# New instruction orders for a fused attention and channel-mixing kernel whose five engine queues are written out as lists

## Chip, cores and metric

The kernel runs on one core of one Trainium2 chip. The metric is the device time of one execution in microseconds (us). TensorE (PE in the profile) multiplies matrices, VectorE (DVE), ScalarE (ACT) and GpSimd (POOL) work elementwise, SyncE (SP) issues nearly all DMAs. Each engine executes its own instruction stream strictly in order; semaphores hold an instruction back until what it reads is there and what it overwrites is no longer needed.

## The reference, cut

```python
B, H, S, D = 8, 8, 576, 64          # batch, heads, positions, head width
scores = matmul(q, k.T) / sqrt(D)
cum = cumsum(log(clip(f, 1e-4, 1)), axis=-1)
scores = where(causal, -1e9, scores + cum[..., :, None] - cum[..., None, :])
attn = softmax(scores)
x = matmul(attn, v)                 # heads side by side: (8, 576, 512)
h = relu(x.T @ w_tok1) @ w_tok2     # mixing over positions, 576 -> 256 -> 576
u = x + h.T
out = u + relu(u @ w_ch1) @ w_ch2   # mixing over channels, 512 -> 1536 -> 512
```

The weights come as 64-bit floats and are turned into pairs of 32-bit parts on the chip ("decoded"). Where the kernel multiplies in the fast 32-bit format it splits a number into a high part and a low rest and adds three products.

## The kernel before

**Attention.** The 64 heads are handled one after the other, two of them (a pair) sharing their loads. Of a pair, q and k come by one DMA (line 670, tile `raw`), and POOL splits them: high part (line 650) and low part (line 658), both into the tile `hl`, of which there is one. SP then gathers each head's operands out of `hl` by three DMAs (lines 713 to 715, recorded as L705, `k<-hl`, 288 KB each): one needs the high part alone, two need both. Two small DMAs a head (line 699, `k<-cc`) add the rows of the running sums. PE makes the score products of 576 positions in three steps (line 732, 754), each into PSUM; DVE adds the mask and takes the extreme (line 739), ACT makes the exponentials (line 746), DVE the reciprocals of the sums (lines 764, 767), POOL divides, five instructions a head (line 774), PE transposes the result (line 788), ACT and DVE copy it out of PSUM in high and low parts (lines 419, 428), one part by way of POOL (line 422), and PE multiplies by the values (lines 856 to 868). The values of a pair come by a DMA (line 678, tile `vr`, two of them), split by ACT (line 648) and POOL (line 658 again, tile `vv`). The first eight heads take shorter ways: their q and k are used unsplit.

**Mixing.** After four heads and after eight of a batch, PE transposes their outputs and mixes over positions (lines 1365 to 1433), and after eight it does the first 256 of the 1536 hidden channels (lines 1463 to 1498), storing `u` (line 1443) and partial sums (line 1498, `pd<-part`) to device memory. These steps are interleaved with the attention of the next heads. After the attention (from about 575 us on) the weights of the other 1280 hidden channels are decoded, mostly on DVE (lines 519 to 579), and multiplied: for 768 tokens directly (lines 1032 to 1068), for the others by a scheme that saves products (lines 1172 to 1292).

**The order.** `build` makes 6091 steps, numbered as they are made; a step is a few instructions of one engine. `ORDER` holds, for each of the five engines, the numbers of its steps in the order in which it executes them (`16:31` is the 31 steps from 16 on). `Plan.run` goes through the five lists with the planner's own costs (`LAT`, the durations given to `op`); a step is taken when it is next on its engine's list, what it reads is there, and a free buffer of each kind that it needs is found. The costs decide which buffer or PSUM bank of a kind a step gets; what each engine does after what is the list's alone. Kinds in `FIFO` are handed out in the order of the steps' numbers.

**Steps that the text names.** 2: the zero row on POOL (line 456). 0 and 1: constant rows on POOL (lines 475, 478). 4, 5, 7: clip, logarithm and running sum of `f` (DVE, ACT, DVE; lines 458, 459, 463). 8, 9: ACT issues the rows of sums of the first two heads (line 443). 10, 11: split of the sums on DVE (lines 468, 469). 16 to 51: filler products of PE (line 491). 53, 54, 55: load, first activation and first DVE step of the first decoded weight tile; 63, 68: steps of the second. 189: load of the first head. 190, 193, 198 and 225, 228, 233: score products of the first two heads; 194, 195, 229, 230: extremes for them; 203, 204: the first head's reciprocals. 612, 613: the first split of q and k on POOL (high, low); 2073, 2074 the one of a later pair, and 1913, 2077 low splits of values. For the pair of 2073: 2078, 2079 small DMAs, 2080, 2081, 2082 gathers (2080 of the high part alone) of its first head; 2124, 2125 and 2126, 2127, 2128 those of its second; 2091, 2086, 2083 the first head's score products.

Of the kernel before, what the change touches and what calls it, by code (L numbers as in the profile page):

```python
# [28 lines left out]
        16:31 198 193 190 47 233 228 48:4 225 266 271 217 212 215 210 219 308 263 303 220:2 252 222 300 247 250 245 254 377 290 255:2 372 285 288 257 283 369 416 421 292 413 293:2 322 327 400 397 389  # L29
        325 295 392 460 329 463 468 320 330 512 331 433 332 507 334 404 337 405 504 436 444 406 441 407 340 480 343:2 448:2 483 491 345 622 630 346 488 625 347 450 348 451 676 668 357 495 353 496 532  # L30
        497 527 498 351 535 671 524 359 539 645 723 642 540:2 728 720 542 653 650 774 688 545 657 548 658 769 696 766 699 691 659 551 660 740 554:5 847 703 559 743 855 850 704:2 751 706 748 562 755
        564 896 786 789 756 901 757 893 568 797 758 570 867 794 948 945 953 583 801 870 802:2 584 804 579 878 875 580 587 994 588 882 913 883 916 924 999 884 991 885 593 598 921 603 608 928 968 929
        976 973 575 965 930:2 807 576 1109 810 980:2 1117 1011 1112 596 1019 1014 982 1022 983 1163 1155 1158 813 816:2 591 1026 1129 1027 1137 1140 1207 1028 1132 818 1029 1215 1210 1175 819:3 601
        606 1144:2 1256 1261 1253 826 832 1032 1035 1038 830 1146 1178 1147 1186 824 1183 1041 1227 1042 1342 1043 1190 1337 1334 1044:2 1238 1191 1046 1235 1230 1192:2 1273 1388 1049 1055 1242 1380
        1276 1284 1243 1383 1281 1244 1051 1057 1245 1070 1066 1440 1354 1432 1288:3 1357 1291 1362 1067 1365 1071 1481 1486 1478 1435 1400 1074 1369 1075 1403 1411 1370 1062 1371 1408 1372 1294 1297
        1063 1452 1415:2 1463 1417 1455 1460 1604 1418 1599 1300 1596 1303:2 1650 1467 1645 1468 1501 1469 1305 1470 1306 1506 1509 1307 1498 1308 1642 1616 1078 1513:2 1627 1624 1619 1083 1515 1697
        1702 1516 1085 1313 1694 1662 1631:2 1665 1670 1748 1673 1633 1080 1743 1740 1319 1519 1088 1093 1634 1317 1714 1311 1090 1677 1522 1725 1717 1678 1095 1829 1722 1525 1679 1821 1680 1824 1528
        1875 1529 1760 1530 1867 1729 1531 1763 1771 1730 1532 1768 1731 1533 1732 1870 1841 1542 1536 1775 1538 1852 1844 1544 1922 1776 1927 1849 1777 1919 1778 1557 1553 1968 1554 1558 1973 1856
        1965 1890 1898 1887 1857:3 1895 1549 1939 1550 1561 1902 1781 1942 1950 1903 1562 1947 1904 1784 1905 2091 2086 1787 2083 1790:2 2137 2132 1954 1792 1996 1955 1793 1956 1794 1988 1993 1957
        1795 1985 2129 2103 1565 2000:2 2114 2111 2106 2002 1572 2184 2189 2003 1570 1800 2181 2149 2118:2 2152 2160 2157 2235 2120 1567 2230 2227 1806 2006 1575 1580 2121 1577 2201 1804 1798 2164  # L40
        2009 2204 2212 2165 1582 2316 2209 2012 2311 2166 2308 2167 2015 2247 2362 2016:3 2216 2019 2250 2258 2217 2354 2255 2218 2020 2219 2357 2328 2023 2029 2262 2025 2331 2339 2031 2414 2263 2409
        2336 2264 2044 2265 2406 2040 2455 2041 2045 2460 2343 2452 2377 2374 2344 2385 2345:2 2382 2036 2426 2037 2048 2389 2268 2437 2429 2390 2049 2434 2391 2271 2392 2573 2578 2274 2570 2277:2
        2624 2619 2441 2279 2475 2442 2280 2443 2281 2480 2483 2444 2282 2472 2616 2590 2052 2487:2 2601 2598 2593 2057 2489 2676 2490 2671 2059 2287 2054 2668 2636 2722 2717 2062 2605 2067 2639 2714
        2647 2291 2606 2064 2644 2607 2285 2608 2293 2688 2493 2496 2069 2651 2499 2652 2691 2803 2699 2696 2653 2795 2654 2798 2734 2502:2 2849 2504:2 2703 2506 2737 2745 2704 2841 2742 2705 2507
        2706 2844 2815 2510 2516 2749 2512 2818 2826 2518 2901 2750 2896 2823 2751 2531 2752 2893 2527 2942 2528 2532 2947 2830 2939 2864 2872 2831 2523 2832 2869 2833 2524 2535 2861 2755 2876 2536
        2924 2916 2877 2758 2921 2878 2913 2879 3065 3060 2761 3057 2764:2 3106 3111 2928 2766 2970 2929 2767 2930 2768 2962 2967 2931 2769 2959 3103 3077 2541 2974:2 3088 3085 3080 2546 2976 3158
        3163 2977 2544 2774 3155 3123 3092:2 3126 3131 3209 3134 3094 2539 3201 3204 2780 2980 2551 2554 3095 2549 3175 2778 2772 3138 2983 3186 3178 3139 2556 3290 3183 2986 3140 3282 3141 3285 2989
        3336 2990 3221 2991 3328 3190 2992 3224 3232 3191 2993 3229 3192 2994 3193 3331 3302 2997 3003 3236 2999 3313 3305 3005 3388 3237 3383 3310 3238 3018 3239 3380 3014 3429 3015 3019 3434 3317
        3426 3359 3348 3351 3318:3 3356 3022 3400 3023 3363 3010 3411 3403 3242 3364 3011 3408 3365 3245 3366 3552 3547 3544 3248 3251:2 3593 3598 3253:2 3415 3590 3449 3416 3457 3417 3255 3454 3418
        3256 3446 3026 3033 3461 3031 3567 3261 3575 3462 3650 3572 3463 3642 3464 3645 3028 3036 3265 3267 3038 3564 3610 3696 3579 3467 3580 3688 3613 3618 3581 3621 3691 3582 3041 3662 3259 3043  # L50
        3470 3473 3777 3625 3769 3673 3665 3626 3772 3627:2 3670 3476 3815 3477 3818 3478:2 3823 3480 3677 3481 3711 3678 3719 3679:2 3486 3484 3716 3492 3723 3490 3800 3792 3724 3708 3797 3725 3875
        3870 3867 3726 3505 3501 3506 3502 3509 3804 3510 3838 3846 3805 3789 3843 3921 3806 3835 3807 3916 3913 3887 3515 3520 3850 3497 3898 3890 3729 3851 3498 3732 3852:2 3895 3513 3518 3933 3902
        3735 3936 3903 3944 3904 3941 3905 3738 3523 3528 3530 3739 3948 3740 3949 3741 3950 3742 3951 3743 3525 3748 3754 3954 3957 3960 3752 3746 3963:6 3971 3977 3973 3979 3984 3988 3996 3992 3989
        3985 3997 3993 4000 4005 4010 4017 4015 4012 4007 4002 4468 4474 4471 4480:2 4477 4482:3 4486 4485 4487 4494 4491 4495:4 4488 4499:3 4505 4512:4 4502 4508:4 4519 4516 4522:9 4533 4536:9 4547
        4550:9 4561 4564:8 4578:8 4572 4575 4586 4589 4592:9 4603 4606 4609 4612 4615 4618 4621 4665 4668 4671 4677 4686 4680 4689 4674 4692 4698 4707 4701 4710 4713 4722 4683 4695 4719 4704 4728
        4716 4725 4731 4734 4737 4740 4743 4749 4746 4752 4755 4758 4761 4764 4804 4767 4808 4812 4816 4820 4831 4835 4839 4843 4847 4856 4860 4864 4868 4872 4880 4884 4888 4892 4911 4896 4915 4919
        4937 4923 4941 4927 4945 4949 4953 5029 5032 5035 4968 5038 4972 5041 4976 5050 4980 5044 4984 5047 5053 5056 5059 5062 5065 5071 5068 5074 5077 5080 5083 5086 5089 5092 5095 5098 5101 5104
        5107 5110 5113 5116 5119 5122 5125 5128 5168 5131 5172 5176 5180 5195 5184 5199 5203 5220 5207 5224 5211 5228 5244 5232 5248 5236 5252 5275 5256 5279 5260 5283 5301 5287 5305 5291 5309 5394
        5313 5332 5317 5336 5397 5340 5400 5344 5403 5348 5406 5409 5415 5412 5418 5421 5424 5427 5430 5433 5436 5439 5442 5445 5448 5451 5454 5457 5460 5463 5466 5469 5472 5475 5478 5481 5484 5487
        5490 5493 5541 5496 5545 5549 5568 5553 5572 5557 5576 5593 5580 5597 5584 5601 5617 5605 5621 5609 5625 5648 5629 5652 5633 5656 5674 5660 5678 5664 5682 5766 5686 5705 5690 5709 5769 5713  # L60
        5772 5717 5775 5721 5778 5781 5787 5784 5790 5793 5796 5799 5802 5808 5805 5811 5814 5817 5820 5823 5826 5829 5832 5835 5838 5841 5844 5850 5847 5853 5856 5859 5862 5865 5905 5868 5909 5932
        5913 5936 5917 5940 5921 5944 5957 5948 5961 5981 5965 5985 5969 5989 5973 5993 6012 5997 6016 6038 6020 6042 6024 6046 6028 6050 6054 6081:2
    """,
# [1683 lines left out]
```

## Time and profile before

| | |
|---|---|
| three runs | 1071.07, 1073.4, 1081.29 us; median 1073.4 |
| profiled execution | 1076.76 us, of it 1075.0 us from the first to the last instruction |
| PE busy | 1032.4 us (96%) |
| DVE, ACT, POOL busy | 869.5, 643.1, 501.3 us |
| mean granted TensorE clock | 0.998 of full speed |

The span is the part of the execution that the profile records; the rest lies around it. A busy PE includes small waits inside its pipeline. In a row such as `[1.90 <-DMA k<-hl]` the engine stood idle for 1.90 us before the instruction and what ended that was a DMA.

### The profile page before, as it was taken

To read this page: it belongs to the slowest core of one execution; us is meant where nothing else is said; L and a number is where in the kernel's file an instruction comes from. 1 tells how busy PE (TensorE), PEld (TensorE's weight loads), DVE (VectorE), ACT (ScalarE), POOL (GpSimd) and SP (SyncE) were. 2 spreads that over 40 slices of the span, in tenths; PEclk is the share of its full clock that TensorE was granted. 3 is DMA by queue.
4 is the path that set the end of the run, shared out by engine and by line. 5 is a ranking of instruction groups with operands and counts; after the bars stand their busy time and mean duration, and the time that the engine had idled before them with its cause. 6 is when DMAs were issued, how large, how long until landed. Compare 5 with 4: busy or idle time off the path is not lost.

```text
span 1075.0 us, 20358 instructions
## 1 busy us (share of the span) xinstructions
PE 1032.4 (96%) x6374; PEld 908.7 (85%) x6374; DVE 869.5 (81%) x2112; ACT 643.1 (60%) x1604; POOL 501.3 (47%) x581
## 2 busy tenths in 40 slices
PE   8997899999999999989899999999999999999998
PEld 5576789899999998989898888878888888888887
DVE  7689888888878877768779899966995995797586
ACT  5778678888788887868778544422631541362142
POOL 6778877867868687768671200002521101102000
PEclk9999999999999999999999999999999999999999
DMA  4548677877777778676864699899899889879874
GB/s 134 158 109 213 170 188 170 255 172 197 197 195 208 179 182 211 155 191 174 218 192 169 217 322 308 270 311 326 281 344 348 239 269 344 282 223 342 244 203 144
DMA packets 138020, 243.36 MB, mean 226 GB/s; under 512 B 20757, under 2 KB 70677, under 8 KB 136889
## 3 DMA queue, kind: packets, MB, share of 16 engines
q1 hardware_dynamic: 137904, 242.05, 77.0%
q8 instruction: 51, 0.84, 0.3%
q14 instruction: 57, 0.46, 0.1%
q10 hardware_dynamic: 8, 0.01, 0.0%
HBM read 145.24 MB, written 46.66 MB: 179 GB/s over the span
## 4 chain that ended last, share of the span: by engine, by line
PE 58%; DMA 14%; DVE 12%; POOL 5%; SPq 4%; ACT 4%; issue 3%; DVEq 0%; POOLq 0%; ACTq 0%
DMA k<-hl 10%; PE bank L1176 5%; PE bank L1178 5%; PE bank L1177 5%; PE bank L732 4%; PE bank L788 4%; PE bank L1242 3%; PE bank L1243 3%; PE bank L1241 3%; PE pair L1241 2%; PE pair L1242 2%; PE pair L1243 2%; PE pair L732 2%; SPq L705 2%; POOL hl L658 2%
## 5 line engine op out<-in xcount | busy, mean ns | idle before, releaser
L774 POOL TENSOR_SCALAR pr<-pr,rec 128x192 f32<-128x192 f32 (+4 forms) x320 | 170.9, 552 | 45.6 <-DVE rec L767 27.0
L419 ACT ACTIVATE p<-bank 128x384 fp32r<-128x384 f32 (+3 forms) x300 | 130.2, 475 | 54.7 <-PE bank L788 50.2
L788 PE MATMUL bank<-ident,pr 128*128 128x128 f32 (+1 forms) x960 | 138.8, 275 | 6.7 <-DVE p L428 1.4
L746 ACT ACTIVATE pr<-bank,nmin 64x64 f32<-64x64 f32 (+3 forms) x256 | 118.4, 469 | 19.2 <-DVE nmin L739 13.4
L428 DVE TENSOR_TENSOR p<-bank,p 128x384 fp32r<-128x384 f32 (+1 forms) x180 | 105.8, 595 | 27.4 <-ACT p L419 26.0
L788 PEld LDWEIGHTS bank<-ident,pr 128*128 128x128 f32 (+1 forms) x960 | 106.7, 131 | 19.8 <-POOL pr L774 4.4
L739 DVE CUSTOM_DVE_ANT_0 bank<-bank,mask 128x448 f32<-128x448 f32 (+3 forms) x256 | 106.3, 433 | 21.1 <-PE bank L732 18.9
L732 PE MATMUL bank<-k 128*128 128x320 f32 (+1 forms) x448 | 79.4, 299 | 13.2 <-DMA k<-hl 10.7
L732 PEld LDWEIGHTS bank<-k 128*128 128x128 f32 x448 | 66.1, 176 | 26.2 <-DMA k<-hl 8.4
L658 POOL TENSOR_TENSOR hl<-raw,hl 128x1152 fp32r<-128x1152 f32 x28 | 74.7, 2667 | 1.0
L868 PE MATMUL pair<-p,vv 128*128 128x512 f32 x240 | 75.0, 318 | 0.0
L419 ACT ACTIVATE hid<-h 128x480 fp32r<-128x480 f32 x76 | 45.7, 606 | 47.7 <-PE bank L1242 27.5
L866 PE MATMUL pair<-p,vv 128*64 128x512 f32 x240 | 71.2, 337 | 0.0
L422 POOL TENSOR_SCALAR p<-low 64x576 fp32r<-64x576 f32 x60 | 41.0, 683 | 58.5 <-DVE low L428 27.3
L1016 POOL TENSOR_TENSOR d_raw<-d_raw 128x256 f32<-128x256 f32 x4 | 2.9, 735 | 122.3 <-DMA d_raw<-ud 122.3
L428 DVE TENSOR_TENSOR low<-bank,p 64x64 fp32r<-64x64 f32 (+1 forms) x120 | 51.8, 441 | 9.7 <-ACT p L419 8.5
L419 ACT ACTIVATE ring<-bank 128x288 fp32r<-128x288 f32 (+2 forms) x96 | 46.7, 498 | 17.4 <-PE bank L1398 5.5
L1194 ACT ACTIVATE h<-bank 128x480 f32<-128x480 f32 x19 | 10.9, 573 | 75.6 <-PE bank L1178 75.6
L425 POOL TENSOR_TENSOR ring<-xt,ring 128x576 fp32r<-128x576 f32 x32 | 46.2, 1453 | 20.8 <-ACT ring L419 20.5
L739 DVE CUSTOM_DVE_ANT_0 pair<-pair,mask 128x576 f32<-128x576 f32 x64 | 48.9, 765 | 8.5 <-PE pair L732 7.4
L419 ACT ACTIVATE st<-h 128x480 fp32r<-128x480 f32 x64 | 38.1, 604 | 23.7 <-PE bank L1242 8.6
L658 POOL TENSOR_TENSOR vv<-vr,vv 128x640 fp32r<-128x640 f32 x30 | 46.9, 1564 | 10.4 <-ACT vv L648 4.9
(357 smaller groups left out, 3466.1 us busy)
## 6 DMA issues: line engine op xcount, KB each, us to landing
pw<-wd SPq DMA_DIRECT2D x280, 256.0 KB
k<-hl SPq DMA_DIRECT2D x168, 288.0 KB
raw<-in_qk SPq DMA_DIRECT2D x28, 576.0 KB
vr<-in_v SPq DMA_DIRECT2D x32, 320.0 KB
d_raw<-in_w_ch SPq DMA_DIRECT2D x80, 128.0 KB
ud<-xt SPq DMA_DIRECT2D x8, 1152.0 KB
pd<-part SPq DMA_DIRECT2D x32, 288.0 KB
wd<-pw SPq DMA_DIRECT2D x20, 384.0 KB
```

Of the source, the lines that this page charges most:

```text
L419: nc.scalar.activation(out, in_, func, scale=scale)
L428: nc.vector.tensor_tensor(out, in_, asf(hi), op=ALU.subtract)
L658: (nc.gpsimd if eng == "POOL" else nc.vector).tensor_tensor(out, in_, asf(hi), op=ALU.subtract)
L732: nc.tensor.matmul(ps[:m, of : of + w], k[:, 0 if fq else 1, i0 : i0 + m], k[:, 1 if fq else 0, j0 : j0 + w], start=(x == 0), stop=(fq or ...
L739: nc.vector.tensor_tensor_reduce(x, x, E["mask"][:m, a : a + w], -1.0 / D**0.5, 3e38, op0=ALU.add, op1=ALU.min, accum_out=E["nmin"][sm][:m ...
L746: nc.scalar.activation(at(pr)[:m, poff[t] : poff[t] + w], at(buf)[:m, of : of + w], AF.Exp, bias=E["nmin"][sm][:m, t : t + 1], scale=-1.0, ...
L774: nc.gpsimd.tensor_scalar(x, x, r, 0.0, op0=ALU.mult, op1=ALU.add)
L788: nc.tensor.transpose(out, at(pr)[:, poff[i] + start[j] : poff[i] + end[j]], E["ident"])
L866: nc.tensor.matmul(x[:D], at(vv)[:, v0 + j, :D], at(pb)[:, 1, c0 : c0 + w], start=False, stop=last)
L868: nc.tensor.matmul(x, at(vv)[:, v0 + j, :], at(pb)[:, 0, c0 : c0 + w], start=False, stop=last)
L1176: nc.tensor.matmul(o, wt[:, 0, :], h_, start=(first and k == 0), stop=False, skip_group_check=True)
L1177: nc.tensor.matmul(o, wt[:, 1, :], h_, start=False, stop=False, skip_group_check=True)
```

## The change

Only the five lists in `ORDER` are different; steps, tiles, buffers, costs and every other line are the same, and each list holds the same numbers as before. Of PE's 1453 steps 743 stand at another place (by at most 22 places), of DVE's 1782 steps 1048 (at most 39), of ACT's 1284 steps 792 (at most 26), of POOL's 576 steps 439 (at most 17), of SP's 996 steps 702 (at most 71). From PE's step 5110 on (about 830 us) nothing is moved. The beginnings of the lists, and on POOL and SP the lines with steps 2073 to 2128:

```diff
     PE="""
-        16:31 198 193 190 47 233 228 48:4 225 266 271 217 212 215 210 219 308 263 303 220:2 252 222 300 247 250 245 254 377 290 255:2 372 285 288 257 283 369 416 421 292 413 293:2 322 327 400 397 389
...
+        16:36 193 190 198 228 233 225 266 271 217 212 263 215 210 219 303 308 220:2 250 222 300 247 252 245 372 377 254 369 255:2 290 285 257 288 283 416 421 292 413 293 327 294 325 295 322 320 392
...
     DVE="""
-        4 7 55:3 64 10 65:2 59 68 73 199 74:2 194:2 191 200 234:2 11 203 77 204 229:2 226 218 82 267 272 91 268 238:2 83 273 216 84 92 264 304 309 86 93 276 310 277 305 253 251 301 95 100:2 313:2 291
...
+        4 7 55:3 10 64:2 59 66 194 191 199 73 200 74 229 195 75 234:2 68 230 203:2 77 226 11 267 272 218 273 82 238:2 83 216 264 268 84 304 309 91 305 92:2 86 251 95 276 310 277 301 253 373 378:2 109
...
     ACT="""
-        5 54 63 8:2 60 72 69 196 192 201 197 202 236 232 81 231 237 78 214 213 90 227 211 269 275 270 6 274 265 312 311 223 87 249 248 306 246 307 99 302 96 108 380:2 286 258 287 375:2 371 364 419
...
+        5 8:2 54 63 60 72 192 201 196:2 202 237 78 231:2 69 236 227 81 213 275 214 6 274 269 211 270 90 265 306:2 311:2 302 87 223 96 249 248 99 108 246 381 380 375:2 114 371 105 258 287 286 420 284
...
     POOL="""
-        0:3 12 58 67 61 13 76 14 70 205 207:2 206 209 15 79 240:2 85 242 244 243 94 282 280 278:2 281 88 97 316 319 103 612 317:2 315 112 386:2 384:2 388 365 115 106 430 429 403 431 428 432 456 121
...
-        2074 1934:5 1901 1980:5 1953 2077 2171:2 2098:5 1999 2117 2144:5 2298 2175 2299 2163 2196:5 2242 1809 2243 1803 2215 2244:2 2396 2246 2397 2323:5 2261 2302 2369:5 2342 2028 2034 2560 2400
...
+        2 0:2 12:3 58 61 67 76 207 206 208 205 209 70 79 244 242 15 241 243 240 85 94 279 612 280 88 282 97 278 281 112 103 115 318 316 319 106 388 317 315 387 385 384 386 365 613 121 432 429 403 428
...
+        1758 1909:2 1815 1840 1836:2 1774 1839 1316 1838 1322 1882 1885 1883 1855 1886 1541 1547 1884 2073:2 1934:2 1901 1938 1937 1936 1913 1980 1984 1981 1953 1982:2 2171:2 2101 2098 2102 2100 2099
...
     SP="""
-        3 53 52 62 71 189 224 80 262 260:2 89 188 298:2 297 611 368 367 98 107 366 410:2 259 412 363 619 116 457 617 459 125 665 663 458 134 454 618 503 501:2 666 621 620 709 143 664 667 614 715 152
...
-        1865:2 1864 1092 1097 1914:3 2075 2072 1917:2 1960:5 1548 2078:3 2173 2124:3 2170 2081:2 2127:2 2176:2 2300 2178 2297 2179:2 2222:2 2225:2 2224 1574 2303:3 2398 1569 2349:2 2395 2306:2 2351:3
...
+        3 53 189 52 224 62 71 611 262 260:2 80 297 299 298 188 259 89 368 98 366:2 107 412 618 411 410 457 116 458 363 459 503 125 502 134 454 619 501 666 621 663 620 667 617 143 709 664 614 665 712
...
+        1820 1864 1819 1862 1908 1865:2 1863 1813 1915 4064 1911 1914 1916:3 1962:2 1961 1964 1960 2072 1087 1097 1092 2075 2080 2126 2079 2128 2125 2081 2127 2124 2078 2082 2170 1548 1082 2178:2
```

On POOL's list of before, 2073 and 1913 stand just ahead of the line that begins with 2074. Loads of q and k are 1908, 2072 and 2170 there, loads of values 1911, 2075 and 2173, stores 1082 to 1097.

## Rows read from the trace of the kernel before

**Rows 1.** The page: busy time of each engine, and the granted TensorE clock in 40 slices.
```profile
PE 1032.4 (96%) x6374; PEld 908.7 (85%) x6374; DVE 869.5 (81%) x2112; ACT 643.1 (60%) x1604; POOL 501.3 (47%) x581
...
PEclk9999999999999999999999999999999999999999
```
**Rows 2.** Windows: stretch, its length, busy us (and instructions) by engine, clock, DMA share, GB/s.
```profile
0.00:25.00 25.00, 20.73 (x128) 13.01 (x129) 18.43 (x58) 12.55 (x34) 16.12 (x28) 1.00 0.51 144
25.00:150.00 125.00, 112.70 (x698) 85.87 (x697) 102.58 (x305) 92.19 (x267) 101.81 (x125) 1.00 0.63 160
150.00:200.00 50.00, 48.64 (x376) 45.87 (x374) 43.26 (x126) 40.61 (x113) 39.92 (x48) 1.00 0.80 200
200.00:560.00 360.00, 347.38 (x2633) 327.38 (x2633) 283.04 (x838) 284.34 (x796) 270.81 (x329) 1.00 0.75 191
...
615.00:700.00 85.00, 83.47 (x480) 73.42 (x479) 83.38 (x190) 39.01 (x74) 0.00 (x0) 1.00 0.91 298
```
**Rows 3.** PE's waits from 200 to 560: total us, times, longest.
```profile
PE bank L732 <- DMA k<-hl: 10.2, 13, 1.9
```
**Rows 4.** PE's waits from 25 to 200, the longest in total.
```profile
PE bank L1397 <- DVE ring L428: 1.7, 1, 1.7
```
**Rows 5.** Timeline of the first 27 us: start, duration, engine, line.
```profile
3.84 1.36 POOL L475 MEMSET xt<- 2x1152 f32 x1 [1.79 <-DVE xt L1650]
...
4.23 0.68 ACT L459 ACTIVATE xt<-xt 64x576 f32<-64x576 f32 x1 [2.20 <-DVE xt L458]
...
5.13 1.05 POOL L478 MEMSET xt<- 2x1152 f32 x1
...
6.24 0.58 POOL L456 MEMSET xt<- 64x576 f32 x1
...
6.47 3.70 PE L491 MATMUL pair<-ident 128*64 128x48 f32 x60
6.85 1.35 DVE L463 TENSOR_TENSOR_SCAN cc<-xt 64x576 f32<-64x576 f32 x1 [2.66 <-POOL xt L456]
...
8.23 1.84 ACTq L443 DMA_DIRECT2D xt<-cc  x2
...
11.39 2.11 PE L732 MATMUL bank<-xt 128*128 128x320 f32 x8 [1.22 <-DVE d_g L531]
```
**Rows 6.** Timeline of POOL around 450 us.
```profile
447.85 1.15 POOL L650 TENSOR_SCALAR hl<-raw 128x1152 fp32r<-128x1152 f32 x1
448.97 1.54 POOL L658 TENSOR_TENSOR vv<-vr,vv 128x640 fp32r<-128x640 f32 x1
450.48 2.67 POOL L658 TENSOR_TENSOR hl<-raw,hl 128x1152 fp32r<-128x1152 f32 x1
```
**Rows 7.** Timeline of PE around 464 us.
```profile
463.49 0.38 PE L732 MATMUL bank<-k 128*128 128x320 f32 x1 [1.90 <-DMA k<-hl]
464.68 0.61 PE L732 MATMUL bank<-k 128*128 128x320 f32 x3 [0.81 <-DMA k<-hl]
```
**Rows 8.** The DMA queue's own waits from 200 to 560.
```profile
SPq L699 <- PE pair L732: 32.7, 9, 6.1
...
SPq L678 <- POOL vv L658: 9.9, 10, 2.9
```
**Rows 9.** Timeline of SP around 280 us.
```profile
279.47 1.21 SPq L699 DMA_DIRECT2D k<-cc  x2
...
282.08 4.00 SPq L705 DMA_DIRECT2D k<-hl  x4
```
**Rows 10.** Chain of work around 285 us.
```profile
282.97 6.85 DMA k<-hl
```
**Rows 11.** Timeline of PE around 290 us.
```profile
289.86 1.14 PE L732 MATMUL bank<-k 128*128 128x320 f32 x7 [0.26 <-DMA k<-hl]
```
**Rows 12.** Chain of work around 460 us.
```profile
455.09 9.54 DMA k<-hl
```
**Rows 13.** Windows: the six us after 464, columns as in rows 2.
```profile
464.00:470.00 6.00, 5.32 (x31) 5.13 (x32) 3.86 (x13) 3.66 (x9) 2.95 (x3) 0.72 0.42 128
```

280 rows, old and new, of tables (ACT, DVE, PE, POOL) are left out of this document.

## The prediction

> **What bounds the kernel now.** I read the page first: TensorE (PE) is busy for 96% of the span at full granted clock [rows 1], and every multiplication stays, so the change can only win or lose PE's idle time and the pace of what PE waits for. The windows by stage come second, and the reader is to see how little idle there is and where [rows 2]: 4.3 us in the first 25, 13.7 us from 25 to 200, 12.6 us from 200 to 560 and 1.5 us from 615 to 700, 32 us together. Third come PE's waits: from 200 to 560 nearly all that has a name is the score product (line 732) waiting for the gathers k<-hl, 10.2 us in 13 waits, the longest 1.9 [rows 3]. From 25 to 200 the longest named wait is 1.7 us, another one each time [rows 4]; there DVE and POOL are busy 83% and 81% of the stretch [rows 2]. From 615 to 700 DVE works 83.4 of 85 us, so that stage ends when DVE's decoding ends, whatever PE does.
>
> **The profiled execution** took 1076.8 us around a span of 1075.0; the median of the three runs is 1073.4. The sum below is made against 1076.8 and its difference carried to the median. One per cent, about what a measurement of this kernel tells from no change, is 10.7 us.
>
> **Part 1, the start.** Before, the zero row (step 2, line 456) stands on POOL behind two memsets that wait for DVE: 3.84 to 6.18, then 6.24 to 6.82; the running sum on DVE (line 463) starts at 6.85, and ACT issues its rows at 8.23 [rows 5]. ACT's logarithm had ended at 4.91. With step 2 first, the sum can start at about 5.0, 1.8 us sooner, and the issue on ACT (now ahead of the two decode activations 54 and 63) likewise. The score that started at 11.39 is then held by the five filler products that now all stand ahead of it, at 0.12 us each (60 rows, two to a step, in 3.70 us: [rows 5]), and by POOL's and DVE's next steps: the decode step 11 (1.3 us) leaves DVE's place ahead of the first softmax sums, steps 68, 229 and 230 come in. The decode activation 54 now waits behind ACT's issue (1.84 us), until 8.2, and the step after the sum on DVE's list, 55, waits for 54: DVE goes on at about 8.7 where it went on at 8.2, which takes 0.5 back. I take 1.8 less 0.5, rounded down to 1.2 us gained, of at most 1.8; none, if the load of the first head lands no sooner. Bounds -1.8 to 0.
>
> **Part 2, the low halves on POOL sooner.** In 13 of the 28 pairs of heads the split of an older pair's values (vv, 1.54 us) stands between the high split (1.15) and the low split of q and k (2.67) [rows 6]; in 6 more it stands just ahead of both. The new list has the two splits side by side in 21 pairs (10 before), with vv mostly six to ten places later. So the last gathers, which need the low split, can be issued 1.5 us sooner, all else kept. If that went straight to PE, every one of the 13 waits would shrink by up to 1.5 us: the waits lie at eleven heads, 2.7 us (1.9 and 0.8, [rows 7]), 2.4, 1.8 and eight under 0.7; 2.3 us would be left, a gain of 7.9. The later vv costs nothing: its reader starts 11 to 23 us after it in the stretch from 200 on, and the places that it gives up are at most 9 us of POOL's work. If that cover were gone, the value products of a head would wait for what is left over. The loads of v move back on SP by up to 23 places; there they waited 9.9 us for POOL to free their buffer, in front of gathers [rows 8].
>
> **Part 3, the gathers on SP crossed.** This goes the other way. SP issues in order, and its small DMAs of the sums (line 699) wait there for a score to free the buffer, 32.7 us in nine waits [rows 8], with everything behind them. Before, the order is head by head. In the new list the gathers of a pair's two heads are mixed: for the pair of step 2073, the first head's last gather (2082) followed directly on 2081; now it stands behind 2128, 2125, 2127, 2124 and 2078. These are two gathers and three small DMAs: gathers were issued four in 4.00 us, with waits, small ones two in 1.21 [rows 9]. So 2082 comes 2 x 1.0 + 3 x 0.6 = 3.8 us later, less the 1.5 of part 2: 2.3 us later. It was on the chain already: issued at 282.97 it took 6.85 us until the score used it [rows 10], where PE stood idle for 0.26 us [rows 11]; with 2.3 us more, PE waits about 2.5 us there. I laid the new order of SP beside the rows of the steps it waits for, head by head from 160 us on. Against its first score the last gather comes sooner for 28 of 47 heads and later for 19, in 13 of them by 1.0 to 4.3 us; the mean is 0.3 us sooner. With the landing time of rows 10, and nothing else gained, the waits would be about 25 us in place of 10.2; with a landing 1.5 us shorter, 18. But the stores of partial sums (line 1498) and the loads of v now stand behind the gathers, where they stood among them when a landing took 9.54 us [rows 12], so landings should get shorter, and a score that waits gives the later ones slack. Parts 2 and 3 together: bounds -7.9 and +15. I take -1.0, near the mean shift and on the side of the emptier queue.
>
> **Part 4, the clock.** After the idle 2.7 us of rows 7 the granted clock fell to a mean of 0.72 from 464 to 470 [rows 13]: 1.7 us of a full clock lost, as 3.4 us at 1.2 GHz instead of 2.4. If that wait shrinks by half the drop may stay away; another head may bring it back. I take -0.8, bounds -1.7 and +1.7.
>
> **Part 5, all other moves.** Half of PE's steps and more of the other lists are permuted, by up to 22 places on PE and 39 on DVE, with no net pull in any stretch of 25 us up to 650 (the mean shift on PE is at most 0.3 us). From 25 to 200, 13.7 us of idle stand to be won; but the same list moves the first split of q and k (612, 613; 3.8 us) in front of softmax divisions at 30 to 60 us, and around 145 to 155 some transposes now come 2 to 4 us sooner on PE and their divisions 1 to 4 us later on POOL. The one against the other: 0, bounds -5 and +5. From 575 to 700 the steps ahead of the decode that PE waits for are the same set on DVE, so that stage only shifts: 0.
>
> **Sum:** -1.2 - 1.0 - 0.8 + 0 = -3.0; 1073.8 for a profiled execution, 1070.4 for the median.
>
> **Rivals.** *A, the low half decides.* Gathers land sooner everywhere since stores and loads of v are out of their way. For it: 10.2 of 12.6 idle us are this one wait. Against it: 19 heads move the wrong way. It gives -7.9 - 1.2 - 1.7 = -10.8: 1062.6. *B, the crossing decides (slower).* Place: SP's queue, at the first head of a pair; price: waits of 18 to 25 us in place of 10.2, less 1.2 from the start, so +7 to +14, 1080 to 1087, middle 1083.5. It decides from the point where a first head's last gather is issued less than its landing time (6.85 in rows 10) before the score. For it: 2082 and its like. Against it: the queue is emptier of stores. The Trainium skill speaks for B: "DMA: Bandwidth & Descriptors", section on queues, rings and completion order, says that each DMA engine consumes one queue's descriptors in ring order, so that a gather put behind five others cannot pass them. By that rule the time is B's; the 9.54 us landing of rows 12 agrees with it as far as one row can. *C, it does nothing:* the moved steps had slack, 1073 within 2 us, since no engine does less work.
>
> **Chances.** The sum's case 0.45, A 0.27, B 0.20, C 0.08. Half of A lies over 1% faster, and 0.05 of the sum's case: 0.19. Half of B is over 1% slower, and 0.03 of part 5 going badly: 0.13. The rest, 0.68, is within 1%. The range reaches into both A and B: 1060 to 1083; the sum's own is 1065 to 1077.
>
> **What would show it.** Right: the sum on DVE (line 463) starts near 5.0 and the first score by 10.9; on POOL the low split follows the high one; k<-hl still holds PE for 6 to 12 us from 200 to 560, at other heads (2091 among them, near 289 us), with no drop near 465. A is right if that wait is under 3 us, B if it is over 17. Wrong altogether: PE idle from 25 to 200 changed by over 5 us, or from 615 on by over 2.

## The result, and the profile after

The changed kernel takes 1057.7 us (median of six runs, 1054.96 to 1058.84) where the kernel before took 1072.93 in the runs beside it (six, 1071.07 to 1081.29): a ratio of 0.9846, 95% interval 0.9811 to 0.988, or 15 us less. The forecast was 1070.4 and the low end of its range 1060.0. The profiled execution took 1058.84 us around a span of 1057.1. Line numbers of after are those of before plus 6.

The page of the changed kernel, busy time and clock (for [rows 1]):

```profile
PE 1028.2 (97%) x6374; PEld 906.0 (86%) x6374; DVE 866.9 (82%) x2112; ACT 644.7 (61%) x1604; POOL 499.7 (47%) x581
...
PEclk9999999999999999999999999999999999999999
```

Its windows by stage (for [rows 2]; after the clock come DMA share and GB/s):

```profile
0.00:25.00 25.00, 21.71 (x129) 13.81 (x129) 18.63 (x60) 12.78 (x36) 15.92 (x29) 1.00 0.55 156
25.00:150.00 125.00, 113.03 (x700) 86.14 (x698) 103.45 (x303) 93.09 (x266) 102.14 (x128) 0.99 0.63 162
150.00:200.00 50.00, 49.91 (x386) 47.31 (x386) 43.36 (x131) 40.99 (x116) 38.04 (x45) 1.00 0.73 187
200.00:560.00 360.00, 355.45 (x2735) 336.30 (x2733) 293.94 (x872) 299.19 (x830) 278.11 (x341) 1.00 0.75 194
...
615.00:700.00 85.00, 84.08 (x465) 73.48 (x464) 80.30 (x178) 36.14 (x68) 0.00 (x0) 1.00 0.93 300
```

PE's idle time from 200 to 560 is 4.6 us where it was 12.6, and 102 more matmuls fit into the stretch. In the list of PE's waits for the same stretch the gathers, 10.2 us in [rows 3], no longer appear by name:

```profile
PE bank L738 <- issue: 1.2, 2, 0.7
PE bank L794 <- POOL pr L780: 0.8, 2, 0.6
PE bank L1469 <- DVE ring L437: 0.6, 1, 0.6
```

The two waits put down to "issue" are what is left of them: they end at 221.89 and 287.13 us, each 0.09 us after the landing of the head's last gather. So 10.2 us became 1.2. The second of them, on PE's timeline:

```profile
286.02 0.39 PE L738 MATMUL bank<-k 128*128 128x320 f32 x1
287.13 1.09 PE L738 MATMUL bank<-k 128*128 128x320 f32 x7 [0.72 <-issue]
```

Why is seen on SP. First a new row of the kernel before, which stands between two of its neighbours in [rows 9]:

```profile
280.73 0.67 SPq L705 DMA_DIRECT2D k<-hl  x1
281.51 0.53 SPq L670 DMA_DIRECT2D raw<-in_qk  x1
```

and the same pair of heads in the changed kernel:

```profile
274.33 1.89 SPq L711 DMA_DIRECT2D k<-hl  x2
276.27 0.64 SPq L705 DMA_DIRECT2D k<-cc  x1
277.09 0.67 SPq L711 DMA_DIRECT2D k<-hl  x1
277.81 0.62 SPq L705 DMA_DIRECT2D k<-cc  x1
278.49 1.35 SPq L711 DMA_DIRECT2D k<-hl  x2
279.88 1.92 SPq L705 DMA_DIRECT2D k<-cc  x2
281.85 0.52 SPq L711 DMA_DIRECT2D k<-hl  x1
282.41 0.59 SPq L676 DMA_DIRECT2D raw<-in_qk  x1
```

Before, the load of the next pair's q and k (576 KB) went out at 281.51, and then the four gathers that need the low half, which PE waited for. Now all gathers go first and the load is issued behind them, at 282.41. Counted over the 27 lists of a pair: before, the load stood ahead of both low-half gathers of the pair's first head in 22 places, now in 3.

The trace also holds every DMA's semaphore increments. The queue's DMAs take eight semaphores in turn, and the last increment before a semaphore's next turn is the moment at which a DMA has landed. Means from issue to landing, from 160 to 550 us:

| | first head's low-half gathers | second head's | all gathers |
|---|---|---|---|
| before | 6.77 us | 6.44 | 6.02 |
| after | 3.98 | 5.05 | 4.39 |

From its last gather's issue a head's first score starts as late as before (7.76 us on the average, 7.70 before); from the end of the low split likewise (11.50, 11.35). What changed is not when a gather is issued but how long it takes: a head's gathers have all landed 2.8 us before its first score on the average, where it was 0.7 before. And they land in the order of the queue: from 160 to 550 us, in both traces and in that of e5 below, no transfer landed ahead of an earlier one except the 4.5 KB ones (38 of 90 of them before).

Where the time was won can be followed by the start of the same PE steps in two traces (median over the steps within 6 us of the place, us against the execution before, minus is sooner):

| place in the trace of before | 45 | 90 | 200 | 300 | 400 | 500 | 560 | 700 |
|---|---|---|---|---|---|---|---|---|
| after | +0.5 | -0.7 | -2.4 | -2.7 | -4.3 | -12.4 | -15.4 | -17.7 |

Some 2 to 3 us of this are the one execution of before: it had the 2.7 us wait and the clock drop of [rows 7, 13], and another run with the same lists up to 570 us stood at -2.5 at 560. Of the 13.0 us that the executions of before and after differ by between 200 and 560, 8.1 are PE's idle time and 1.7 the clock drop; the rest lies inside what counts as busy and is not explained here.

### The profile page after: what moved, and what is told of

It reads as the page before. It is cut to its first block, busy times and chain, and to the rows that moved or that the text cites. A ratio compares the mean times of both kernels' runs of the same rounds, so it can differ in the third digit from the quotient of the medians.

```text
span 1057.1 us, 20264 instructions
## 1 busy us (share of the span) xinstructions
PE 1028.2 (97%) x6374; PEld 906.0 (86%) x6374; DVE 866.9 (82%) x2112; ACT 644.7 (61%) x1604; POOL 499.7 (47%) x581
## 4 chain that ended last, share of the span: by engine, by line
PE 73%; DVE 15%; DMA 5%; ACT 3%; issue 2%; POOL 2%; SPq 1%; DVEq 0%; POOLq 0%; ACTq 0%
PE bank L794 8%; PE bank L738 6%; PE bank L1182 4%; PE bank L1183 4%; PE bank L1184 4%; PE bank L1248 3%; PE bank L1249 3%; PE bank L1247 3%; PE pair L738 3%; PE pair L872 2%; PE pair L874 2%; PE pair L1247 2%; PE pair L1248 2%; PE pair L1249 2%; PE bank L1403 2%
## 5 line engine op out<-in xcount | busy, mean ns | idle before, releaser
L780 POOL TENSOR_SCALAR pr<-pr,rec 64x64 f32<-64x64 f32 (+4 forms) x320 | 170.2, 547 | 61.3 <-DVE rec L773 37.5
L752 ACT ACTIVATE pr<-bank,nmin 128x320 f32<-128x320 f32 (+3 forms) x256 | 118.5, 468 | 28.3 <-DVE nmin L745 24.6
L738 PE MATMUL bank<-k 128*128 128x320 f32 (+1 forms) x448 | 76.2, 296 | 3.5 <-issue 1.2
L874 PE MATMUL pair<-p,vv 128*128 128x512 f32 x240 | 72.0, 316 | 0.0
L434 DVE TENSOR_TENSOR low<-bank,p 64x512 fp32r<-64x512 f32 (+1 forms) x120 | 52.5, 444 | 21.2 <-ACT p L425 19.3
L1275 POOL TENSOR_TENSOR d_raw<-d_raw,d_g 128x480 f32<-128x480 f32 x11 | 14.6, 1324 | 108.8 <-DMA d_g<-ud 55.9
```

Of the source, the lines that this page charges most:

```text
L434: nc.vector.tensor_tensor(out, in_, asf(hi), op=ALU.subtract)
L738: nc.tensor.matmul(ps[:m, of : of + w], k[:, 0 if fq else 1, i0 : i0 + m], k[:, 1 if fq else 0, j0 : j0 + w], start=(x == 0), stop=(fq or ...
L752: nc.scalar.activation(at(pr)[:m, poff[t] : poff[t] + w], at(buf)[:m, of : of + w], AF.Exp, bias=E["nmin"][sm][:m, t : t + 1], scale=-1.0, ...
L780: nc.gpsimd.tensor_scalar(x, x, r, 0.0, op0=ALU.mult, op1=ALU.add)
L874: nc.tensor.matmul(x, at(vv)[:, v0 + j, :], at(pb)[:, 0, c0 : c0 + w], start=False, stop=last)
```

## The experiments

All ratios are to the kernel before in the same runs, with 95% intervals. A run's line numbers are those of its own file.

**e1 to e4: one list at a time.** e1, kernel before, SP (the same in 27 places):

```diff
-2124 2125 2126 2170 2081 2082 2127 2128
+2124 2125 2126 2081 2082 2127 2128 2170
```

> The kernel before; on SP's list alone the load of the next pair's q and k (line 670, 576 KB) is put behind the last of the four gathers that need the low half, in all 27 places (before it stood ahead of all four in 22). Theory 'load in front': the gathers landed 6.0 us after their issue on the average from 160 us on, 4.4 in the changed kernel, because that load no longer goes first; so here the landing falls to about 4.5, the 13 waits k<-hl of 10.2 us fall under 3 us and the time is 1062 to 1066. Theory 'split order' (POOL's values split out of the way makes the gain): nothing is won here, 1071 to 1075. Theory 'only all lists together': 1071 to 1075 too, with waits elsewhere.

Measured: 1.0011 (0.9995 to 1.0028). The landing did what was expected (mean 4.42 us over all gathers), k<-hl fell only to 6.0 us, and the time not at all. POOL tells why; its waits from 200 to 560:

```profile
POOL hl L649 <- DMA pd<-part: 7.5, 3, 2.9
POOL hl L649 <- DMA k<-cc: 5.2, 3, 2.6
...
POOL hl L649 <- DMA k<-hl: 3.9, 3, 2.1
POOL hl L649 <- PE pair L731: 2.9, 1, 2.9
```

and PE's in the same stretch:

```profile
PE bank L731 <- DMA k<-hl: 6.0, 6, 1.6
PE pair L855 <- POOL p L421: 1.5, 1, 1.5
```

The high split now waits some 20 us (the semaphores named are shared by several DMAs). By the landings it started within 0.4 us of the load's in 8 of 22 pairs; before in none, with 6.7 us to spare in the median. The load had been moved too far, and POOL, which executes in order, handed the delay on.

e2, changed kernel, SP (21 places):

```diff
-2080 2126 2079 2128 2125 2081 2127 2124 2078 2082 2170
+2080 2126 2079 2170 2128 2125 2081 2127 2124 2078 2082
```

> The changed kernel; on SP's list alone the load of the next pair's q and k is put back ahead of as many low-half gathers as in the kernel before (21 places). Theory 'load in front': gathers land after about 6 us again, k<-hl holds PE for 7 us or more from 200 to 545, time 1064 to 1070. Theory 'split order': waits stay under 2 us and the time at 1057 to 1060.

Measured: 0.9958 (0.9931 to 0.9984), some 11 us over the changed kernel's 0.985. The first heads' gathers took 6.41 us again, and from 170 to 560 PE waited for them and for the small DMAs of the sums:

```profile
PE bank L738 <- DMA k<-hl: 5.8, 4, 2.8
PE bank L738 <- DMA k<-cc: 2.7, 2, 2.1
```

From 200 on k<-hl is 3.0 us of this, where 7 or more were expected, but PE's idle time from 200 to 560 is 10.4 us, 4.6 in the changed kernel. So the load's place is needed for the gain; theory "split order" falls.

e3, kernel before, POOL (11 places):

```diff
-2073 1913 2074
+2073 2074 1913
```

> The kernel before; on POOL's list alone the split of values is moved from between the high and the low split of q and k to behind the low one, in 11 places from step 1587 on. Theory 'split order': k<-hl falls from 10.2 to about 2.5 us, time 1064 to 1067. Theory 'load in front': the load of the next pair, which waits for the same low split, is sooner too and stays in front, so the landing stays at 6 us; the issue is up to 1.5 us sooner in 11 pairs, which leaves 4 to 7 us of the waits: 1067 to 1071.

Measured: 1.0258 (1.023 to 1.0287), which neither theory had. SP's waits from 200 to 560:

```profile
SPq L677 <- POOL vv L657: 36.0, 13, 5.7
```

In [rows 8] this was 9.9 us. The load of values stands in front of gathers and waits for the buffer that the later split frees, so gathers are held up; the low split's 1.5 us are lost many times over.

e4, the kernel before with SP's whole new list:

> The kernel before with the whole SP list of the changed kernel, and nothing else changed. Theory 'load in front': the landing falls to about 4.5 us and most of the waits with it, 1062 to 1068. The prediction's rival B (crossed gathers on SP wait in turn) would show here at its purest, since nothing else is sooner: waits of k<-hl over 17 us, 1078 to 1087. Theory 'only all lists together': slower than before by some us, with waits spread over many lines.

Measured: 1.0475 (1.0442 to 1.0508). Slow, but not by rival B: gathers land after 4.31 us, and PE's longest wait from 200 to 560 is for ACT:

```profile
PE bank L790 <- ACT part L1498: 10.5, 2, 6.8
```

and ACT's longest is for the loads of values, which the new list puts behind gathers, while ACT's old list asks for them early:

```profile
ACT vv L650 <- DMA vr<-in_v: 30.5, 7, 8.2
```

Theory "only all lists together" is right for SP's whole list.

**again, e5 to e7.** The changed kernel once more:

> The changed kernel as it is, beside the kernels of the same runs: 0.98 to 0.99 of the kernel before under every theory.

Measured: 0.9849 (0.982 to 0.9877). e5, kernel before, SP (22 places), the load only two gathers later:

```diff
-2170 2081 2082 2127 2128
+2081 2082 2170 2127 2128
```

> The kernel before; on SP's list alone the load of the next pair's q and k is put between the low-half gathers of the first head and those of the second (22 places). With the load behind all four (the first run) gathers landed after 4.4 us and k<-hl fell to 6.0 us, but POOL's high split waited some 20 us for the later load and handed the loss on. Theory 'load in front, with POOL's slack kept': the load is only two gathers later (2 us of a slack of 6.7 us in the median), so the first head's gathers land after about 4.5 us, POOL's high split waits under 6 us, and the time falls by 4 to 8 us, to 0.992 to 0.996 of before. Theory 'only all lists together': within 0.3% of before or slower.

Measured: 0.9929 (0.9903 to 0.9955), 7.6 us of 1073.8. The first heads' gathers land after 3.90 us, the second heads', which have time, after 6.09. On SP, the pair that was shown above (of the first three gathers one is the second head's of the high part, two are the first head's):

```profile
281.10 2.17 SPq L704 DMA_DIRECT2D k<-hl  x3
283.32 1.28 SPq L669 DMA_DIRECT2D raw<-in_qk  x1
284.65 1.92 SPq L704 DMA_DIRECT2D k<-hl  x2
```

Its window of 200 to 560:

```profile
200.00:560.00 360.00, 356.81 (x2755) 340.61 (x2754) 293.40 (x879) 298.07 (x834) 278.04 (x342) 1.00 0.75 198
```

What held PE there for the gathers, and what held POOL's high split:

```profile
PE bank L731 <- DMA k<-hl: 0.4, 1, 0.4
```

```profile
POOL hl L649 <- DMA k<-hl: 6.7, 9, 1.9
POOL hl L649 <- DMA k<-cc: 1.1, 1, 1.1
POOL hl L649 <- PE bank L787: 0.8, 1, 0.8
POOL hl L649 <- PE pair L731: 0.3, 1, 0.3
```

PE is busy for 356.8 of 360 us, 355.5 in the changed kernel, with one step moved per pair. POOL's high split waits 8.9 us in all, where under 6 were expected, but no longer for the load (4.1 us to spare in the median, 1.5 at the least).

e6, changed kernel, SP: each pair's gathers head by head in the places they have (`2080 2081 2079 2082 2125 2126 2127 2124 2078 2128 2170`).

> The changed kernel; on SP's list alone the gathers of each pair are put head by head into the same places of the list (the first head's three first), so that the prediction's crossing is undone. If crossing costs what the prediction's part 3 says (a first head's last gather 2 to 4 us later), this is faster by 2 us or more than the changed kernel; if the small DMAs and the landing decide, it is within 2 us of it; if the mixed order follows when k tiles come free, it is slower, as gathers wait in front of others.

Measured: 0.9865 (0.9836 to 0.9894) beside 0.9849: not faster. With the load in its new place, crossing the gathers costs nothing that shows; the intervals are some 3 us wide to either side.

e7, the kernel before with the new order of all lists from 200 to 570 us:

> The kernel before with the changed order of all five lists for the steps that started between 200 and 570 us, the rest as before. By the two traces this stretch won 12.6 of 17.9 us, 2.8 came before 200 and 2.2 behind 570: so 0.987 to 0.991 of before if the stretches are independent; 0.996 or more if the gain from 200 on was inherited from the order before 200.

Measured: 0.9933 (0.9908 to 0.9957), a little less than the two traces had promised, and the same as e5: the whole reordering of this stretch brings what the one load brings.

**e8 to e11: the other stretches.** e8, the new order before 200 us alone:

> The kernel before with the changed order of all five lists for the steps that started before 200 us, the rest as before. The two profiled executions differ there by 2.8 us; the first load of a next pair that stood in front of a first head's gathers comes only from step 1100 on (124 us). If these 2.8 us are the list's and are kept, 0.996 to 0.998 of before; if they were given back later, where gathers decide, 1.000. The prediction's parts 1 and 5 took 1.2 us for this stretch.

Measured: 0.9959 (0.9927 to 0.999), at the edge of what was expected; PE's steps at 200 us came 2.2 us sooner in its trace. e9, the new order behind 570 us alone:

> The kernel before with the changed order for the steps that started behind 570 us alone. The two profiled executions differ there by 2.2 us, DVE being the busiest engine of the stretch from 615 to 700. If the order of DVE's decoding makes that, 0.997 to 0.999 of before; if it was only carried over from the attention part, 1.000. The prediction's part 5 took 0.

Measured: 0.9987 (0.9952 to 1.0022): not told from nothing. e10, the new order before 200 and behind 570, and between them the old one with e5's edit (20 places):

> The kernel before with the changed order before 200 and behind 570 us; between them the order of before, with the load of the next pair's q and k behind the first head's low-half gathers as the single edit (20 places). If the load in front is the whole gain of the stretch from 200 to 570, this equals the changed kernel: 0.983 to 0.987 of before. If the other moves of that stretch (POOL's splits, stores and loads of values, transposes) bring a part, it stays at 0.988 or more.

Measured: 0.9859 (0.981 to 0.9907); within the interval this is the changed kernel (0.9849). As far as this interval and e7 tell, from 200 to 570 the other moves aren't needed for the gain.

e11, changed kernel, POOL (10 places, `1909 1910 1815` becomes `1909 1815 1910`):

> The changed kernel; on POOL's list alone the split of an older pair's values is put back between the high and the low split of q and k in 10 of the places where before had it, so the low split ends up to 1.5 us later. If the low split's place decides (the prediction's part 2), waits of k<-hl come back by up to 0.8 us in each of 10 pairs, 0.988 to 0.992 of before; if the gathers now have slack, within 2 us of the changed kernel, 0.983 to 0.987.

Measured: 1.016 (1.011 to 1.0211), far worse than either. POOL's longest wait from 200 to 560, and PE's:

```profile
POOL vv L664 <- ACT vv L654: 19.5, 7, 7.5
```

```profile
PE pair L862 <- POOL p L428: 12.8, 3, 6.5
```

POOL's low split of the values needs ACT's high split of the same values, and that stands where the new lists have it: near 272 and 504 us it began as soon as the load of the values had landed, in the other waits of POOL about 2 us or more behind that, when ACT's own list came to it. Put early, the low split waits on POOL, with all of POOL's list behind it. In both kernels the place of this split fits the places of its load and of ACT's split; it can't be moved alone (e3, e11).

**e12 to e14: the start and 25 to 200.** e12, changed kernel, PE:

```diff
-46:6 193 190 198 228 233 225
+46 193 190 198 47 228 233 48:4 225
```

> The changed kernel; on PE's list alone the last five filler products (steps 47 to 51) go back behind the first score products, where before had them. In the profiled executions of the changed order the first score started at 11.27 to 12.12 us, the later the later the clock had risen, though the sum was 1.83 us sooner; with the old order it was 11.39 each time. If the fillers ahead hold it, the first score now starts before 11.3 whatever the clock, and steps near 45 us of the old trace come 0.5 to 1.5 us sooner than in the changed kernel; if the landing of the rows of sums holds it, it stays at 11.3 to 12.1. In the whole time at most 1.5 us, 0.982 to 0.987 of before.

Measured: 0.9818 (0.9778 to 0.9858). Two rows of PE's timeline:

```profile
11.28 1.25 PE L738 MATMUL bank<-xt 128*128 128x448 f32 x4 [0.95 <-DMA xt<-cc]
...
25.16 1.07 PE L862 MATMUL pair<-part,vr 64*64 64x512 f32 x2 [0.42 <-DMA vr<-in_v]
```

The first score starts at 11.28 as expected, but steps near 45 us stand at +0.5, no sooner than in the changed kernel, where runs with all fillers ahead and a clock that rose as early (e10 at 5.3 us, e11 at 5.6; this run at 5.6) stand at -0.4. So a first score that is sooner doesn't make the start sooner. Of the 0.9 us the row above shows 0.42, the first value product's wait for its load of values; the rest stays open.

e13, e12 with the load behind the first head's low-half gathers in the last three places (`3144 3053 3055 3098 3052 3099 3056` becomes `3053 3055 3098 3052 3099 3056 3144`):

> The kernel of the run before this one, and on SP's list the load of the next pair's q and k behind the first head's low-half gathers in the three places where the changed order still has it in front (1196, 3144, 3856). If the load in front costs about 0.35 us in a place (7.6 us in 22), 1 us is won: 0.981 to 0.986 of before, the fastest of all.

Measured: 0.9826 (0.9789 to 0.9862), 1056.94 us beside 1056.71 of e12: the expected 1 us doesn't show, nor could it in an interval of 4 us to either side. It beats the kernel before, and isn't told apart from the changed one.

e14, the new order from 25 to 200 us alone:

> The kernel before with the changed order for the steps that started between 25 and 200 us alone. If the gain before 200 us lies here (the prediction's part 5 took 0 with bounds of 5 us), the steps near 200 us come 2.5 to 4.5 us sooner than in the kernel before, with a clock drop near 93 us counted in, and the time is 0.995 to 0.998 of before. If it is the start's, they come at the same time, and the time is 1.000.

Measured: 0.9967 (0.9938 to 0.9996), steps at 200 us 2.9 us sooner with two clock drops of 3.4 us counted in. As far as e8 (0.9959) and this run tell, the gain before 200 us lies here and not in the start.

## Why the prediction was wrong

The direction was right, the size not: 3.0 us forecast, 15 measured. And the direction was in part luck, since two of the three terms that made it, the start and the clock, brought little or nothing. By its own steps:

**Part 3, the step that failed.** "With the landing time of rows 10, and nothing else gained, the waits would be about 25 us in place of 10.2; with a landing 1.5 us shorter, 18." A landing was carried over as if it belonged to the gather, and it belongs to what stands in front of it in the queue. The part counted gathers, small DMAs, stores and loads of values on SP, and left out the largest DMA of a pair, the 576 KB load of q and k, which stood ahead of just the gathers in question, at 281.51 in the rows of before. The list moved it behind them, and the first heads' landing fell by 2.8 us (6.77 to 3.98), where the part let delays of 1.0 to 4.3 us in 13 heads run into waits. At its own example, 2082, PE waits 0.7 us (the row put down to "issue" above) where 2.5 were forecast. Crossing itself costs nothing that shows (e6). Parts 2 and 3 together stood at -1.0; e5 shows -7.6 for the load alone and e7 -7.2 for the whole stretch, near the bound of -7.9 that the prediction had and didn't take.

**Rival B's rule.** The order in the queue did decide. The Trainium skill's rule ("DMA: Bandwidth & Descriptors", queues, rings and completion order: each DMA engine takes a ring's descriptors in order) agrees with the order of the landings above and with e5, 6.77 against 3.90 us for the same gathers with and without the load ahead. The prediction applied it to 288 KB gathers among themselves and not to the load of twice their size.

**Rival A** had the outcome (waits for gathers under 3 us, "gathers land sooner everywhere"; its 1062.6 us are 5 short) but named stores and loads of values as what goes out of the way. As an estimate that spreads each DMA evenly from its issue to its landing, averaged over the gathers, 232 KB of the q and k load were still under way ahead of a gather at its issue before, and 82 after; stores and loads of values together 41 before and 43 after.

**Part 2.** The low split does follow the high one, but no score starts sooner after it (11.50 us from its end, 11.35 before). "The later vv costs nothing" holds only beside the new SP list: without it SP waited 36.0 us for it (e3).

**Part 1.** The sum starts at 5.02, as forecast, but the first score at 12.12 instead of 10.9 at the latest. The part let the score move with the issue of the rows of sums and held it on PE by the five fillers, 0.12 us each (0.13 measured, 70 rows in 4.54 us); what failed is that the rest was taken to move along. The fillers began later, at 7.65 us and not at 6.47, since the mask products ahead of them ran longer at the lower clock, and ended at 12.19. And the two DMAs of the rows, issued 1.78 us sooner (6.45 and 7.72), had landed only 0.17 us sooner (11.02 for 11.19). With an early rise of the clock (11.21 in e10, 11.27 in e2) or the fillers put back (11.28 in e12) that landing holds the score, which starts 0.25 us behind it in each of the three (0.95 us of waiting in e12), so 0.1 to 0.2 us was there to be won at the score. Near 45 us the old start with the new order behind it stands at +0.3 (e14), the new start with all fillers ahead at -0.4 to +0.5, the later the later the clock rose. The start is thus worth 0.7 us at most and nothing with a late rise, where 1.2 was taken.

**Part 4.** The drop near 465 is gone, and another came at 93 us among PE's idle 0.4, 0.7 and 1.1 us (90 to 94 us), as the caveat on "another head" had it; the six us there:

```profile
92.00:98.00 6.00, 4.52 (x22) 4.01 (x22) 5.37 (x14) 4.53 (x14) 5.70 (x8) 0.72 0.34 113
```

Nothing was won where -0.8 was taken.

**Part 5** took 0 with bounds of 5. From 25 to 200 it was -3.5 (e14's 0.9967, whose interval reaches from 0.4 to 6.7 us); which of its moves made it stays open. Behind 570 the two traces differ by 2.3 us (-15.4 to -17.7), and e9 can't tell that from nothing.

Beyond the load, e8 and e9 stand at 4.4 and 1.4 us; with e5's 7.6 that is 13.4 of 15, each with an interval of 3 to 4 us to either side, and e10 has them together.

## What to carry to other kernels

A DMA's time to landing is not its own: before carrying one over to a new order, list what stands ahead of it in the queue, the large prefetch first of all. A prefetch with slack goes behind the transfers that an engine is about to wait for, but only as far as its own slack reaches: two gathers later won 7.6 us here, four later nothing. In lists that execute in order an instruction, the DMA that feeds or frees its buffer and the step of another engine between them are tied: moved alone beyond the slack between them, they won nothing (e1) or lost (e3, e11).

## What the runs showed of the hardware

PE's first product started at 1.84 or 1.85 us in each execution, but the granted clock rose from 1.2 to 2.4 GHz anywhere between 4.98 and 8.24 us (one mask product takes 1.06 us ahead of the rise and 0.59 behind it), so that the same six mask products took 4.2 to 5.5 us. Two runs, e2 and the changed kernel:

```profile
2.23 4.21 PE L1623 MATMUL bank<-mask,ident 128*128 128x512 f32 x6
```

```profile
2.23 5.49 PE L1623 MATMUL bank<-mask,ident 128*128 128x512 f32 x6
```

The clock rose at 5.03 us in the first and at 8.24 in the second. The old start hid this (first score at 11.39 or 11.40 in each run that begins with all the old lists), the new one doesn't (11.21 to 12.12).

From 160 to 550 us the mean landing of a gather followed the KB that were under way ahead of it at its issue, counted as what had been issued less what the DMA packets had moved: 662 KB and 6.02 us before, 581 and 5.59 in e2, 515 and 4.91 in e5, 395 and 4.39 after. The other 13 traces lie between 379 KB with 4.31 us (e4) and 688 with 6.08 (e3).
